# The factors of one elimination step side by side in SBUF instead of 128 bytes apart, in the 32 x 32 inverses of a chunked recurrence

## Chip, cores and metric

One core of one Trainium2 chip. The metric is the device time of one execution in microseconds (us), from the first to the last instruction of the kernel and what little lies around them; less is better.

## What is computed

A recurrence over 768 time steps (4 batches x 8 heads, head size 40), then two feed-forward blocks on its 3072 output rows.

```
for t in range(768):                       # per batch b and head h, state is 40 x 40
    y[t]  = r[t] @ state
    Sa    = state @ a[t]
    state = state * w[t][None, :] - outer(Sa, b[t]) + outer(v[t], k[t])
x = y as rows of 320
x = layer_norm(h * softmax(h)) * g_ln @ w_out        # h = x @ w_in, 1024 wide
out = leaky(x @ w_in2) @ w_out2                      # 2048 wide, slope alpha below 0
```

## The kernel before

The recurrence is cut into 24 chunks of 32 time steps. Within a chunk the steps depend on each other through a strictly lower triangular 32 x 32 matrix per batch and head; the kernel builds these matrices (`gen1`), inverts one plus them, and uses the inverses as matmul operands. Six calls of `inverse(W)`, W = 0 to 5, invert four chunks each: 128 triangular matrices of 32 x 32, of which every partition holds one, 1024 floats long. A chunk has a slot in the program; `slot(g)` writes down the recurrence's stages in a fixed order (`stage_x`, `stage_u`, `stage_uf`, `stage_st`, `stage_g2`, `stage_s`, `stage_y`), and strews work of other chunks between them: transposes (`trans`), `gen1` of later chunks, decoding of weights (`decode`), the first feed-forward block (`mm1`, `soft`, `mm2`) in a queue of TensorE work.

The order of TensorE's instructions is written out by hand, from tables of expected waits (`WT`) and expected durations; the other engines take theirs in the order of the program as the tile scheduler places it. Each engine runs its instructions in that order.

`inverse(0)` runs alone ahead of slot 0. `inverse(W)` for W = 1 to 5 has 33 pieces, a start, 31 steps and an end. The first 18 pieces are strewn over the slot g = 4W - 2, the rest over g = 4W - 1. The result is read by `stage_u` (L442) and `stage_uf` (L465) of the slots 4W to 4W + 3. So `stage_u` of slot 4W waits for the end piece.

- The start (L366) is a block transpose on VectorE (DVE): it reads `lraw`, laid out [row s][chunk and pair][column t] over partitions, and turns it so that each partition has one matrix `NT`.
- Step s adds to every row i <= s of the growing inverse `M` a multiple of the factors of that step: `M[i, t] += M[i, s] * NT[t, s]` for t > s. It is done as a product into `tmp` (L354) and a sum (L358), each over (s + 1) x (31 - s) elements, which is 87 elements at s = 2 and s = 28, 256 at s = 15. In the product the first operand is one word of `M` per row, repeated along the row, and the second is the list of factors, repeated for every row. The first two and the last two steps go another way (L383), with scalars from `NT` or `M`.
- The end (L387) is a second block transpose, of `M`, into the memory of `NT`.
- With W = 0, DVE takes only the rows below 10 and POOL the rest (`pool_rows`), and each product and sum on DVE is cut in two. With W > 0, DVE takes all rows; POOL only clears `M` and sets its diagonal (L132, L133).

Other instructions of DVE that come up below, in its order among the inverse's: L482 (state sums out of `pst`), L508 (`KBS` sums), L544 (`Yt`, the chunk's output out of `py`), L580 and L582 (the softmax of the first block), L620 (`lnl`).

Of the kernel before, what the change touches and what calls it, by code (L numbers as in the profile page):

```python
# [48 lines left out]
def tile_kernel(ctx: ExitStack, tc: tile.TileContext, w_fm, a0_fm, a_fm, kb_fm, r_fm, v_fm, v_tm,  # L49
                w1_in, w1_out, g_ln, w2_in, w2_out, alpha, ident_d, mask_d, r, k, v, w, a, b, w1_nat, out,  # L50
                manual=True):
    nc = tc.nc
# [78 lines left out]
    def unit(M, eng):  # L131
        eng.memset(M, 0.0)  # L132
        eng.memset(M.rearrange("p a b -> p (a b)")[:, ::33], -1.0)  # L133
# [22 lines left out]
    st = {}  # L156
# [185 lines left out]

    def inverse(W):
        M, NT = LMN[2 * W % 3], LMN[(2 * W + 1) % 3]

        P = PR[W > 0]

        def rank1(eng, tmp, s, rows):
            nt = 31 - s
            l = NT[:, s + 1:32, s]  # L350
            tv = tmp[:, 0:sum(b - a for a, b in rows) * nt].rearrange("p (i t) -> p i t", t=nt)
            for a, b in rows:
                sh = [128, b - a, nt]
                eng.tensor_tensor(out=tv[:, a - rows[0][0]:b - rows[0][0]], in0=M[:, a:b, s:s + 1].to_broadcast(sh),  # L354
                                  in1=l.unsqueeze(1).to_broadcast(sh), op=ALU.mult)
            for a, b in rows:
                o = M[:, a:b, s + 1:32]
                r = eng.tensor_tensor(out=o, in0=o, in1=tv[:, a - rows[0][0]:b - rows[0][0]], op=ALU.add)  # L358
            return r

        def pool_rows():
            for s in range(P, 31):
                rank1(nc.gpsimd, b1.tile([128, TM], F32, name="tmp2", tag="Yt"), s, [(P, s + 1)])

        def start():
            nc.vector.transpose(out=NT, in_=st["lraw", W].rearrange("p l t -> p t l"))  # L366
            if W:
                unit(M, nc.gpsimd)
            pool_rows()

        def step(s):
            n, nt = min(s + 1, P), 31 - s
            m = n // 2
            if n <= SM:
                ops = [(M[:, i, s + 1:32], NT[:, s + 1:32, s], M[:, i, s:s + 1]) for i in range(n)]
            elif nt <= SM:
                ops = [(M[:, 0:n, s + 1 + i], M[:, 0:n, s], NT[:, s + 1 + i, s:s + 1]) for i in range(nt)]
            else:
                st["step"] = rank1(nc.vector, b1.tile([128, 256], F32, name="tmp"), s,
                                   [(0, m), (m, n)] if W == 0 else [(0, n)])  # L380
                return
            for o, x, f in ops:
                st["step"] = nc.vector.scalar_tensor_tensor(out=o, in0=x, scalar=f, in1=o, op0=ALU.mult,  # L383
                                                            op1=ALU.add)

        def fin():
            st["fence"] = nc.vector.transpose(out=NT.rearrange("p l t -> p t l"), in_=M.rearrange("p i t -> p t i"))  # L387
            st["NT", W] = NT

        yield 1.1, start  # L390
        for s in range(31):
            yield 0.15 + 2 * (s + 1) * (31 - s) / 960.0, (lambda s=s: step(s))
        yield 1.1, fin
# [402 lines left out]
    def inv_tasks(g):  # L796
        W, c4 = divmod(g, 4)
        if 2 * W + 3 >= NW or c4 < 2:
            return []
        inv = [f for _, f in inverse(W + 1)]  # L800
        return inv[:NI] if c4 == 2 else inv[NI:]
# [115 lines left out]
    def phase1():  # L917
# [23 lines left out]
        for i, (_, f) in enumerate(inverse(0)):  # L941
            f()
            if i == KSTEP:
                with tc.issue_after(st["step"].ins):
                    nc.vector.memset(busy[:, 0:1], 0.0)  # L945
# [403 lines left out]
```

## Time and profile before

| | before |
|---|---|
| median of 3 runs | 1167.23 us (1165.36 to 1168.53) |
| the profiled execution, its own time | 1166.42 us |
| its span, first to last instruction | 1164.6 us |
| TensorE (PE) busy | 978.9 us (84%) |
| VectorE (DVE) busy | 811.2 us (70%) |
| ScalarE (ACT) busy | 520.4 us (45%) |
| GpSimd (POOL) busy | 503.7 us (43%) |
| mean granted TensorE clock | 0.901 of full speed |

A busy share is a mean over the whole span; the second feed-forward block (the last 410 us) is almost all TensorE, the stretch before it is mixed. The rows further down take single stretches.

### The profile page before, as it was taken

The numbers are of one execution on the slowest core, as the hardware profiler recorded it, in microseconds if no ns is written. First come the engines' busy times: TensorE is split into PE (matmuls) and PEld (weight loads), VectorE is DVE, ScalarE is ACT, GpSimd is POOL, SyncE is SP. The second block draws the span as 40 slices with busy tenths as digits, with TensorE's granted clock in tenths as the row PEclk, the third lists the DMA queues.
The fourth block names the chain that finished last, engine by engine and source line by source line (L and its number), as shares of the span: only waits on it lengthen the run. The fifth ranks groups of instructions, "written<-read, shape, count | busy, mean of one in ns | idle before, by whom it ended". The sixth has DMA issues, their size and how long they took to land.

```text
span 1164.6 us, 37097 instructions
## 1 busy us (share of the span) xinstructions
PE 978.9 (84%) x15934; PEld 808.5 (69%) x15934; DVE 811.2 (70%) x1610; ACT 520.4 (45%) x1198; POOL 503.7 (43%) x546
## 2 busy tenths in 40 slices
PE   7275687588878978888787878889999999999997
PEld 3143354467666767666676667778989999999997
DVE  8898689978997798779977976656533333333343
ACT  3325454476537653755475547556312121212121
POOL 6858455444434442443344234436233333333333
PEclk8687987789888887988888889999999999999999
DMA  7513343334333433343333342443402020201000
GB/s 161 149 53 85 99 137 113 99 104 120 106 97 107 122 80 96 90 100 111 99 85 88 101 135 71 117 141 133 124 2 61 8 62 7 62 6 41 6 23 15
DMA packets 104543, 99.52 MB, mean 85 GB/s; under 512 B 38068, under 2 KB 83764, under 8 KB 104372
## 3 DMA queue, kind: packets, MB, share of 16 engines
q1 hardware_dynamic: 104372, 97.07, 30.6%
q8 instruction: 127, 2.08, 0.8%
q14 instruction: 44, 0.36, 0.1%
HBM read 71.62 MB, written 25.43 MB: 83 GB/s over the span
## 4 chain that ended last, share of the span: by engine, by line
PE 47%; DVE 29%; POOL 7%; issue 6%; ACT 5%; DMA 5%; SPq 0%; POOLq 0%; DVEq 0%; ACTq 0%
PE ph L1015 15%; DVE tmp L354 5%; PE h L575 5%; PE acc L1035 5%; PE acc L1033 5%; PE acc L1034 5%; DVE LMN L358 4%; DMA kbf<-in_kb_fm_dram 4%; DVE VUS L482 2%; DVE KBS L508 2%; PE pf L465 2%; POOL XS L312 2%; DVE H L277 2%; PE po L628 1%; PE pu L442 1%
## 5 line engine op out<-in xcount | busy, mean ns | idle before, releaser
L1022 POOL TENSOR_TENSOR gll<-gt,gh 128x512 fp32r<-128x512 f32 (+1 forms) x112 | 129.0, 1152 | 224.0 <-ACT gh L1021 222.9
L595 DVE TENSOR_SCALAR gt<-ph,al 128x512 f32<-128x512 f32 (+1 forms) x112 | 75.4, 673 | 189.8 <-PE ph L1015 189.6
L1021 ACT CAST gh<-gt 128x512 fp32r<-128x512 f32 (+1 forms) x112 | 62.5, 559 | 254.5 <-DVE gt L596 212.6
L575 PE MATMUL h<-w1h,xt 128*128 128x512 f32 x240 | 105.2, 487 | 16.3 <-ACT h L584 16.3
L312 POOL TENSOR_TENSOR XS<-XS,H 40x512 f32<-40x512 f32 (+1 forms) x48 | 66.6, 1392 | 92.7 <-DVE H L277 55.8
L354 DVE TENSOR_TENSOR tmp<-LMN,LMN 128x87 f32<-128x87 f32 (+25 forms) x189 | 95.0, 514 | 3.4
L1033 PE MATMUL acc<-w2h,gh 128*128 128x320 f32 x288 | 89.0, 309 | 0.0
L1034 PE MATMUL acc<-w2l,gh 128*128 128x320 f32 x288 | 89.0, 309 | 0.0
L1035 PE MATMUL acc<-w2h,gll 128*128 128x320 f32 x288 | 88.9, 309 | 0.0
L528 POOL TENSOR_TENSOR YS<-YS,mask 64x512 f32<-64x512 f32 x48 | 64.0, 1333 | 49.0 <-ACT YS L527 47.2
L211 PE MATMUL busy<-busy 128*128 128x512 bf16 x221 | 66.4, 455 | 19.5 <-DVE busy L945 18.2
L358 DVE TENSOR_TENSOR LMN<-LMN,tmp 128x87 f32<-128x87 f32 (+25 forms) x189 | 76.3, 415 | 2.7
L596 DVE SCALAR_TENSOR_TENSOR gt<-ph,gt 128x512 f32<-128x512 f32 (+1 forms) x112 | 68.8, 615 | 3.7
L575 PE MATMUL h<-w1l,xt 128*128 128x512 f32 x144 | 68.6, 476 | 0.0
L575 PEld LDWEIGHTS h<-w1h,xt 128*128 128x128 f32 x240 | 50.3, 221 | 26.0 <-ACT h L584 18.5
L628 PE MATMUL po<-wo1h,lnh 128*128 128x320 f32 x192 | 67.1, 349 | 0.5 <-DVE lnl L620 0.5
L630 PE MATMUL po<-wo1h,lnl 128*128 128x320 f32 x192 | 61.9, 322 | 0.0
L629 PE MATMUL po<-wo1l,lnh 128*128 128x320 f32 x192 | 61.8, 322 | 0.0
L1015 PE MATMUL ph<-w1h,w2h 128*128 128x512 f32 x180 | 59.3, 394 | 0.0
L211 PEld LDWEIGHTS <-busy 128*128 128x128 bf16 x221 | 22.9, 112 | 49.7 <-DVE busy L945 18.3
L326 PE MATMUL pg<-XS,kbf 104*32 104x64 f32 x1536 | 38.5, 239 | 22.0 <-DVE kbf L303 12.8
L581 ACT ACTIVATE P<-h,sm 128x1024 f32<-128x1024 f32 x24 | 26.7, 1114 | 65.1 <-DVE sm L580 62.1
(200 smaller groups left out, 2743.5 us busy)
## 6 DMA issues: line engine op xcount, KB each, us to landing
kbf<-in_kb_fm_dram SPq DMA_DIRECT2D x24, 416.0 KB
x2d<-x SPq DMA_DIRECT2D x24, 320.0 KB
xd<-Y SPq DMA_DIRECT2D x24, 256.0 KB
xt<-xd SPq DMA_DIRECT2D x12, 512.0 KB
raw<-in_w_in_dram SPq DMA_DIRECT2D x20, 256.0 KB
wt<-in_w_fm_dram SPq DMA_DIRECT2D x24, 211.7 KB
raw<-in_w_in_dram SPq DMA_DIRECT2D x8, 512.0 KB
raw<-in_w_out_dram SPq DMA_DIRECT2D x16, 256.0 KB
```

What stands on the lines that cost most here:

```text
L211: nc.tensor.matmul(st["busy"], lhsT=busy[:, 0:128], rhs=busy, start=True, stop=True)
L312: (nc.vector if w < 2 and e in DA else nc.gpsimd).tensor_tensor(out=o, in0=o, in1=h, op=ALU.mult)
L354: eng.tensor_tensor(out=tv[:, a - rows[0][0]:b - rows[0][0]], in0=M[:, a:b, s:s + 1].to_broadcast(sh), in1=l.unsqueeze(1).to_broadcast(sh) ...
L358: r = eng.tensor_tensor(out=o, in0=o, in1=tv[:, a - rows[0][0]:b - rows[0][0]], op=ALU.add)
L575: nc.tensor.matmul(st["h"][:, ns], lhsT=l, rhs=r, start=j == 0, stop=j == len(ops) - 1)
L595: nc.vector.tensor_scalar(out=tmp, in0=h, scalar1=0.0, scalar2=al, op0=ALU.min, op1=ALU.mult)
L628: nc.tensor.matmul(po, lhsT=lh[:, k], rhs=wo1h[:, k], start=k == 0, stop=False)
L1015: nc.tensor.matmul(p, lhsT=l, rhs=r, start=j == 0, stop=j == len(ops) - 1)
L1022: nc.gpsimd.tensor_tensor(out=gll, in0=t, in1=f32(gh), op=ALU.subtract)
L1033: nc.tensor.matmul(acc, lhsT=gh[:, cs], rhs=oh, start=f == 0, stop=False)
L1034: nc.tensor.matmul(acc, lhsT=gh[:, cs], rhs=ol, start=False, stop=False)
L1035: nc.tensor.matmul(acc, lhsT=gll[:, cs], rhs=oh, start=False, stop=f == K2 - 1)
```

## The change

`NT` as an object in memory keeps its place and size. A view `N` with the two inner dimensions exchanged takes its place in the start and in the steps: the start's transpose writes matrix element [t][s] to word 32 s + t in place of word 32 t + s. The factors `N[:, s+1:32, s]` of one step are then 31 - s neighbouring words; before, they were 31 - s words with 32 words from one to the next. The end piece writes the result as before, and nothing else differs: on every engine the same instructions stand in the same order.

```diff
     def inverse(W):
         M, NT = LMN[2 * W % 3], LMN[(2 * W + 1) % 3]
+        N = NT.rearrange("p s t -> p t s")
...
         def rank1(eng, tmp, s, rows):
             nt = 31 - s
-            l = NT[:, s + 1:32, s]
+            l = N[:, s + 1:32, s]
...
         def start():
-            nc.vector.transpose(out=NT, in_=st["lraw", W].rearrange("p l t -> p t l"))
+            nc.vector.transpose(out=N, in_=st["lraw", W].rearrange("p l t -> p t l"))
...
             if n <= SM:
-                ops = [(M[:, i, s + 1:32], NT[:, s + 1:32, s], M[:, i, s:s + 1]) for i in range(n)]
+                ops = [(M[:, i, s + 1:32], N[:, s + 1:32, s], M[:, i, s:s + 1]) for i in range(n)]
             elif nt <= SM:
-                ops = [(M[:, 0:n, s + 1 + i], M[:, 0:n, s], NT[:, s + 1 + i, s:s + 1]) for i in range(nt)]
+                ops = [(M[:, 0:n, s + 1 + i], M[:, 0:n, s], N[:, s + 1 + i, s:s + 1]) for i in range(nt)]
```

## Rows read from the trace of the kernel before

**Rows 1.** The whole chain that ended last, by line; and the page's product group.

```profile
by line: PE ph L1015 14.8%; issue 6.1%; DVE tmp L354 5.5%; PE h L575 4.7%; PE acc L1035 4.7%; PE acc L1033 4.7%; PE acc L1034 4.7%; DVE LMN L358 4.4%; DMA kbf<-in_kb_fm_dram 3.6%; DVE VUS L482 2.0%; DVE KBS L508 1.8%; PE pf L465 1.7%; POOL 
...
L354 DVE TENSOR_TENSOR tmp<-LMN,LMN 128x87 f32<-128x87 f32 (+25 forms) x189 | 95.0, 514 | 3.4
```

**Rows 2.** Stretches with inverses: length, busy us by engine, clock, DMA (W 0, 1, 2, 3, 5).

```profile
core 0: us, PE busy (x) PEld busy (x) DVE busy (x) ACT busy (x) POOL busy (x), PEclk, DMA share, GB/s
36.00:69.00 33.00, 9.69 (x99) 4.49 (x100) 31.70 (x121) 6.60 (x21) 23.20 (x57) 0.64 0.37 95
161.00:225.00 64.00, 42.09 (x836) 27.89 (x833) 60.88 (x117) 23.98 (x56) 29.20 (x29) 0.73 0.37 105
284.00:336.00 52.00, 41.16 (x963) 33.17 (x965) 49.75 (x105) 28.57 (x70) 19.35 (x25) 0.90 0.38 99
398.00:453.00 55.00, 44.21 (x937) 36.36 (x939) 49.44 (x105) 28.48 (x69) 19.34 (x25) 0.84 0.37 92
...
635.00:689.00 54.00, 43.43 (x1014) 35.13 (x1009) 49.47 (x105) 28.18 (x69) 17.77 (x22) 0.86 0.41 110
```

**Rows 3.** TensorE's longest waits, 250 to 700 us: total, times, longest.

```profile
PE pu L442 <- DVE LMN L387: 18.3, 4, 5.4
...
PE px L429 <- DVE Yt L544: 9.7, 4, 2.7
```

**Rows 4.** Products and sums at s = 15, inverses 2 to 5: busy, mean ns.

```profile
L354 DVE TENSOR_TENSOR tmp<-LMN,LMN 128x256 f32<-128x256 f32 x4 | 2.5, 616 | 0.1
...
L358 DVE TENSOR_TENSOR LMN<-LMN,tmp 128x256 f32<-128x256 f32 x4 | 1.7, 426 | 0.1
```

**Rows 5.** DVE's order of time, inverse 2, s = 2, 27 and 28: start us, us.

```profile
288.95 0.30 DVE L354 TENSOR_TENSOR tmp<-LMN,LMN 128x87 f32<-128x87 f32 x1
...
330.48 0.37 DVE L354 TENSOR_TENSOR tmp<-LMN,LMN 128x112 f32<-128x112 f32 x1
330.88 0.28 DVE L358 TENSOR_TENSOR LMN<-LMN,tmp 128x112 f32<-128x112 f32 x1
331.19 0.25 DVE L354 TENSOR_TENSOR tmp<-LMN,LMN 128x87 f32<-128x87 f32 x1
331.48 0.25 DVE L358 TENSOR_TENSOR LMN<-LMN,tmp 128x87 f32<-128x87 f32 x1
```

**Rows 6.** The two block transposes, by line: duration ns min/median/max.

```profile
L366 DVE STREAM_TRANSPOSE LMN<-LMN x6: 1918/1982/2003, 36.1 to 635.9; 128x1024 f32<-128x1024 f32 x6
...
L387 DVE STREAM_TRANSPOSE LMN<-LMN x6: 1972/2017/2029, 66.0 to 685.8; 128x1024 f32<-128x1024 f32 x6
```

**Rows 7.** Order of time, inverse 2: TensorE's pst and py, DVE's L482 and L544.

```profile
313.54 1.42 PE L477 MATMUL pst<-VUS,KBS 64*40 64x40 f32 x64
...
315.30 0.49 DVE L482 TENSOR_TENSOR VUS<-pst,VUS 40x320 f32<-40x320 f32 x1
...
323.77 1.42 PE L540 MATMUL py<-YS,KBS 104*40 104x32 f32 x64
...
326.75 0.68 DVE L544 TENSOR_TENSOR Yt<-py,H 104x512 f32<-104x512 f32 x1
```

**Rows 8.** Waits of DVE in inverse 3, and of TensorE in inverse 1.

```profile
DVE Yt L544 <- PE py L540: 1.9, 1, 1.9
...
PE h L575 <- ACT h L584: 11.4, 1, 11.4
```

**Rows 9.** Order of time in inverse 0: DVE and POOL together.

```profile
52.08 0.66 DVE L354 TENSOR_TENSOR tmp<-LMN,LMN 128x85 f32<-128x85 f32 x2
52.66 0.62 DVE L358 TENSOR_TENSOR LMN<-LMN,tmp 128x85 f32<-128x85 f32 x2
...
51.85 0.52 POOL L354 TENSOR_TENSOR tmp<-LMN,LMN 128x121 f32<-128x121 f32 x1
52.45 0.57 POOL L358 TENSOR_TENSOR LMN<-LMN,tmp 128x121 f32<-128x121 f32 x1
```

## The prediction

> **What bounds the kernel now.** I read the chain of work that ended last first, to see whether the edited lines lie on it at all. They do [rows 1]: the products (L354) hold 5.5% of the span, 5.5% of 1164.6 = 64 us, out of 95.0 us that DVE spends on them in the whole run. So two thirds of what they cost is on the path, by this view.
>
> Next, the stretches in which inverses run [rows 2]. The reader is to see DVE's busy time against the length: 31.70 of 33 us in inverse 0, 60.88 of 64 in inverse 1, 49.75 of 52 in inverse 2, 49.44 of 55 in inverse 3, 49.47 of 54 in inverse 5. DVE is the engine that hardly ever idles there, while TensorE, which carries the next stages, is busy for some 80% of inverses 2 to 5, 66% of inverse 1.
>
> Third, what TensorE waits for in that part [rows 3]. It waits 18.3 us in four times at `pu` for the inverse's end piece, and 9.7 us in four times at `px` for `Yt`, which stands in DVE's order behind the first half of the inverse. Both waits end with a DVE instruction that has inverse steps ahead of it. In inverse 1 the wait has another name but the same cause [rows 8]: 11.4 us at `h` for ACT's L584, which needs DVE's L582, which stands behind the end piece.
>
> **The price of the 128-byte step.** The sum of a step (L358) works on as many elements as its product (L354), with neighbouring words in all operands. At s = 15 the two take 616 and 426 ns [rows 4]: 190 ns more for 256 elements, 0.74 ns each. The difference could come from the second operand (128-byte steps) or from the first (one word repeated along a row). Three rows speak for the second. At s = 27 (rows of 4 factors) product and sum take 0.37 and 0.28 us, 0.8 ns per element; at s = 28 (rows of 3 factors) 0.25 and 0.25 [rows 5]: with three factors read over and over the price is gone, though the first operand is repeated there as everywhere. And the start's transpose reads 1024 elements in 128-byte steps with no operand repeated, and takes 1982 ns [rows 6]. From the sums, 256 elements in 426 ns and 87 in 250, an element without the price takes 1.04 ns, so 1024 would take 426 + 768 x 1.04 = 1225; the 757 ns on top are 0.74 ns per element, the same price. So I charge 0.74 ns per element to the 128-byte read, for s = 2 to 27.
>
> [...]
>
> **What the change removes.** One inverse with W > 0 has 5187 product elements in s = 2 to 27 (the sum of (s + 1)(31 - s)); at 0.74 that is 3.84 us of DVE time, 19.2 us over five. What of it reaches the end differs by place. In inverse 2:
>
> - Before `Yt` of the first slot, s = 2 to 8: 1064 elements, 0.79 us. TensorE waits at `px` for this `Yt`, 9.7 / 4 = 2.4 us each time [rows 3], so all of it counts.
> - s = 9 to 18: 2455 elements, 1.82 us. Here TensorE runs beside DVE: `pst` ends at 313.54 + 1.42 = 314.96 and DVE takes it up at 315.30 [rows 7]. DVE could come 0.34 us earlier before it waits for TensorE. Counted: 0.34, and the other 1.48 us turn into idle time of DVE.
> - s = 19 to 27: 1668 elements, 1.24 us, in front of the end piece, for which TensorE waits 18.3 / 4 = 4.6 us [rows 3]. The second `Yt` stands among them, and its `py` is ready at 325.19, 1.56 us before DVE comes to it [rows 7]; the 0.94 us of the steps s = 19 to 24 ahead of it fit in that. Counted: all 1.24.
>
> That makes 2.4 us. Inverse 5 has the same look, 2.4. In inverse 3 DVE already waits 1.9 us for `py` at that second `Yt` [rows 8], so of the last part only the steps behind it count, s = 25 to 27 (403 elements, 0.30 us): 0.79 + 0.34 + 0.30 = 1.4. Inverse 4, whose rows I don't show, lies between, 2.0. In inverse 1 DVE is busy in all but 3 of 64 us and TensorE waits much; of 3.84 I count 2.4, since decoding of weights, which also needs ACT, POOL and transfers, shares the stretch. Sum: 2.4 + 2.4 + 1.4 + 2.0 + 2.4 = 10.6 us.
>
> **Inverse 0.** DVE has at most 10 rows: 3534 elements in s = 2 to 27, at 0.74 2.6 us, and nothing else runs on DVE. But product and sum differ little while POOL works beside it: two products of 85 elements take 0.66 us, two sums 0.62 [rows 9], 0.04 us for 170 elements, 0.24 ns each, 0.8 us in all. Something of POOL's, whose own product of 121 elements lasts 0.52 us in the same time, covers most of the price. Between 0.8 and 2.6 I take 1.3, nearer to the row of the same place. POOL's products read the factors too; their 0.52 against 0.57 us of the sums shows no price, so I count nothing (at 0.74 on its 1771 elements, the sum of (s - 9)(31 - s) for s = 10 to 30, 1.3 us would be the other end).
>
> **What it adds.** The start's transpose now writes in 128-byte steps as well as it reads so. The end piece does both already and takes 2017 ns against 1982 [rows 6]: 0.035 us, six times, 0.2 us (0.7 us by the extremes, 2029 against 1918). The steps of L383 read factors in the first two steps only, 91 elements in an inverse, 0.07 us less: nothing. No wait, buffer or transfer is added, and no order changes.
>
> **Sum.** 10.6 + 1.3 - 0.2 = 11.7 us off the profiled execution's 1166.42, 1154.7. The median of before lies 0.8 us above that execution, so 1155.5. Bounds: all of 19.2 + 2.6 on the path gives 1167.2 - 21.8 = 1145.4; only the steps ahead of the first `Yt` and behind the second in inverses 2 to 5, 4 x (0.79 + 0.30) = 4.4 us, gives 1162.8.
>
> **The rivals.**
>
> *The repeated word pays as well* (8%). Then the price hangs on the first operand, the products stay at 616 ns, and the time stays at 1167.2 or 0.2 above, for the transposes. For it: the rows of s = 15 and s = 27 fit it as well. Against it: s = 28, and the transposes. [...]
>
> *TensorE closes the gap* (10%). DVE's time falls by 19 us, but the stages' matmuls take over as the bound: what `pu` gains is waited for again further on in the slot, and only the gain at `px` is left, 4 x 0.79 = 3.2 us, 1164.0. For it: in inverses 2 to 5 TensorE is busy for 80% already, and the middle steps gain next to nothing. Against it: the waits at `px` and `pu` are 2 to 5 us each, larger than what is taken from them.
>
> *The clock eats it* (6%), which ends slower. [...]
>
> **How the numbers follow.** My forecast, a gain of 4 to 18 us, has 76%: 1149 to 1163. The first two rivals together stand at 18%, the slower one at 6%. The likeliest is 1155.5; the range 1149 to 1163.5 holds about 8 in 10. A difference under 0.3% (3.5 us) can't be told from none on this kernel. Faster by more: 0.80, since some of the second rival ends just beyond. Within: 0.13. Slower: 0.07.
>
> **What would show it.** The product at 256 elements falls from 616 to about 430 ns (by the first rival it stays above 600), that of 87 elements at s = 28 stays at 0.25 us, that at s = 2 falls from 0.30 to 0.25. The start's transpose stays near 2.0 us. DVE's busy time falls by about 20 us, and DVE shows new idle time at L482 of the second slots, some 1.5 us each, which is where the rest of the price went. TensorE's wait at `pu` falls by 1 to 1.5 us each time, that at `px` by 0.8. From slot 20 on (680 us before) everything stands 11 to 12 us earlier, and the last 410 us are as before. I am wrong in the price if the products don't fall to the sums' level; in the path if they do and the time doesn't follow; in inverse 0 if its DVE stretch of 32 us loses less than 0.8 or more than 2.6 us.

## The result and the profile after

The changed kernel takes 1148.59 us (median of 6 runs, 1143.54 to 1149.97) against 1166.11 for the kernel before beside it: ratio 0.985, interval 0.9817 to 0.9884, so 17.5 us less. A second series of it gave 0.984 (0.9804 to 0.9876). The forecast was 11.7 us less and a range down to 1149.0. The direction and the price of the step hold; the size was too small. Of the 6.9 us between the forecast time, 1155.5, and 1148.59, 1.1 us is the base: the forecast started from a median of 1167.23. The profiled execution took 1149.97 us with a span of 1148.2, against 1166.42 and 1164.6.

All line numbers behind L343 are one higher than before. First the page of the changed kernel, busy time by engine, and its two groups of products and sums.

```profile
PE 976.5 (85%) x15913; PEld 810.8 (71%) x15934; DVE 790.7 (69%) x1610; ACT 519.9 (45%) x1198; POOL 496.7 (43%) x546
...
L359 DVE TENSOR_TENSOR LMN<-LMN,tmp 128x87 f32<-128x87 f32 (+25 forms) x189 | 75.9, 413 | 2.7
L355 DVE TENSOR_TENSOR tmp<-LMN,LMN 128x87 f32<-128x87 f32 (+25 forms) x189 | 71.9, 392 | 3.4
```

The products fell from 95.0 us [rows 1] to 71.9, 23.1 us less, below the sums. DVE's busy time as a whole fell by 20.5. The grouped rows of s = 15 show the price gone to the last element, and the order of time in inverse 2 shows the ends of the row lengths (s = 2, and s = 27 and 28); these answer to [rows 4] and [rows 5].

```profile
L355 DVE TENSOR_TENSOR tmp<-LMN,LMN 128x256 f32<-128x256 f32 x4 | 1.7, 426 | 0.1
L359 DVE TENSOR_TENSOR LMN<-LMN,tmp 128x256 f32<-128x256 f32 x4 | 1.7, 424 | 0.1
```

```profile
285.92 0.23 DVE L355 TENSOR_TENSOR tmp<-LMN,LMN 128x87 f32<-128x87 f32 x1
...
324.84 0.28 DVE L355 TENSOR_TENSOR tmp<-LMN,LMN 128x112 f32<-128x112 f32 x1
325.15 0.28 DVE L359 TENSOR_TENSOR LMN<-LMN,tmp 128x112 f32<-128x112 f32 x1
325.46 0.25 DVE L355 TENSOR_TENSOR tmp<-LMN,LMN 128x87 f32<-128x87 f32 x1
```

616 ns became 426, with the first operand a repeated word as before; 0.37 us became 0.28 where a row has four factors, and 0.25 stayed 0.25 where it has three. So the repeated word costs nothing here: the product that has it takes 426 ns, the sum that has none 424. The 128-byte step was the whole price.

The same stretches as in [rows 2], from the start piece to the end piece:

```profile
core 0: us, PE busy (x) PEld busy (x) DVE busy (x) ACT busy (x) POOL busy (x), PEclk, DMA share, GB/s
38.00:67.00 29.00, 8.88 (x96) 4.03 (x98) 27.55 (x120) 6.46 (x20) 18.52 (x50) 0.59 0.37 98
161.00:222.00 61.00, 40.62 (x801) 28.66 (x802) 56.10 (x117) 23.76 (x56) 26.83 (x29) 0.70 0.39 110
281.00:330.00 49.00, 40.24 (x972) 32.86 (x974) 45.89 (x105) 28.33 (x70) 19.01 (x25) 0.93 0.41 104
393.00:442.00 49.00, 41.02 (x947) 33.48 (x948) 45.68 (x105) 28.50 (x69) 19.06 (x25) 0.91 0.40 103
622.00:671.00 49.00, 40.15 (x944) 32.52 (x942) 45.44 (x102) 27.39 (x66) 16.85 (x22) 0.90 0.43 119
```

DVE's busy time falls by some 4 to 5 us in each stretch, with as many instructions as before, give or take three. TensorE's share of its stretch rises a little (40.24 of 49 us in inverse 2, 41.16 of 52 before). The clock in inverses 2, 3 and 5 is higher in this execution (0.93, 0.91 and 0.90 against 0.90, 0.84 and 0.86), in inverses 0 and 1 lower (0.59 and 0.70 against 0.64 and 0.73).

TensorE's waits, to be read beside [rows 3]:

```profile
PE pu L443 <- DVE LMN L388: 16.5, 4, 4.9
...
PE px L430 <- DVE Yt L545: 8.9, 4, 2.4
```

They fell by 1.8 and 0.8 us in total; the prediction wanted 4 to 6 and 3.2. Both ends of the wait moved: in inverse 2 the end piece stands 2.6 us closer to the start piece (the table of stretches below), yet the wait for it lost about 0.5, so TensorE comes to it earlier too. The experiments bear this out: the total at `pu` is 17.9 to 18.4 us in the six profiles in which the late steps, from s = 19 on, have the 128-byte step, and 16.1 to 16.5 in the eight in which they read neighbours, whatever the earlier steps do. So here the change in a wait's length is no gauge of what a faster releaser is worth.

The last 410 us are as before: TensorE is busy for 397.06 us of them at a clock of 0.99 now, for 397.15 at 1.00 before. Of the inverse's instructions the start piece alone got longer, by 0.13 us in the median (1982 ns [rows 6] to 2111):

```profile
L367 DVE STREAM_TRANSPOSE LMN<-LMN x6: 2077/2111/2203, 38.3 to 622.7; 128x1024 f32<-128x1024 f32 x6
```

### The profile page after: what moved, and what is told of

It reads as the page before. It is cut to its first block, busy times and chain, and to the rows that moved or that the text cites. A ratio compares the mean times of both kernels' runs of the same rounds, so it can differ in the third digit from the quotient of the medians.

```text
span 1148.2 us, 37076 instructions
## 1 busy us (share of the span) xinstructions
PE 976.5 (85%) x15913; PEld 810.8 (71%) x15934; DVE 790.7 (69%) x1610; ACT 519.9 (45%) x1198; POOL 496.7 (43%) x546
## 4 chain that ended last, share of the span: by engine, by line
PE 49%; DVE 29%; ACT 6%; issue 6%; POOL 5%; DMA 4%; SPq 0%; DVEq 0%; POOLq 0%; ACTq 0%
PE ph L1016 15%; PE h L576 5%; PE acc L1036 5%; PE acc L1035 5%; PE acc L1034 5%; DVE LMN L359 4%; DVE tmp L355 3%; DMA kbf<-in_kb_fm_dram 3%; DVE VUS L483 2%; DVE H L277 2%; PE pf L466 2%; DVE KBS L509 2%; DVE XS L336 2%; DVE kbf L303 1%; PE pg L326 1%
## 5 line engine op out<-in xcount | busy, mean ns | idle before, releaser
L211 PE MATMUL busy<-busy 128*128 128x512 bf16 x200 | 60.1, 454 | 24.6 <-DVE tmp L355 19.6
L355 DVE TENSOR_TENSOR tmp<-LMN,LMN 128x87 f32<-128x87 f32 (+25 forms) x189 | 71.9, 392 | 3.4
```

The source lines that it names most:

```text
L211: nc.tensor.matmul(st["busy"], lhsT=busy[:, 0:128], rhs=busy, start=True, stop=True)
```

## The experiments

Apart from `again` and `v_rows`, all of these take the changed kernel and put the 128-byte step back for chosen steps, inverses or engines. Only the products change (L355 of the changed kernel); the few scalar steps (L384) stay as changed. The products then read words of the same tile that lie across the diagonal, so these kernels compute with other factors; sizes, strides and order are those of the kernels compared. The edit is one line and a condition:

```diff
+    def old(W, s, eng):
+        return W > 0 and 9 <= s <= 18          # u_mid; the others differ here alone
...
-            l = N[:, s + 1:32, s]
+            l = (NT if old(W, s, eng) else N)[:, s + 1:32, s]
```

**The changed kernel once more (again), no edit.**

> The changed kernel once more, to know its time better and to have a second profile. If chance of the runs made the gap between 11.7 us forecast and 17.5 measured, this comes out near 1154; if not, near 1148.6 again. The stretch of inverse 0 is 28.3 us long again, the lengths of the slots with the second halves of inverses 1 to 5 vary between 24 and 29 us.

1148.8 us, 0.984 (0.9804 to 0.9876). Chance of the first series is out; the forecast was too small. The stretch of inverse 0 is 28.5 us in this profile.

**All products put back, the start as changed (u_all): `return True`.**

> The changed kernel with the 128-byte step put back in all products of all inverses (values differ, sizes and order are the same); only the start's transpose still writes in 128-byte steps, as changed. If nothing but the products' reads made the gain, this is the time of the kernel before plus six times 0.12 us for the longer start, 1166.8. If the four parts put back one by one (about 11 us by their medians) are all that there is, 1148.6 + 11 = 1159.6.

1165.97 us, 0.9997 (0.9974 to 1.0020). So the reads of the products are the whole gain, to within the 2.7 us of the interval, and the longer write of the start can't be seen in the time. This kernel computes with other factors than the kernel before and takes the same time, so the values don't disturb these comparisons by more than that. The four parts put back singly, below, come to some 10 us by their medians but to 2.3%, 26 us, by their ratios: time alone can't add them up.

**Inverse 0 put back (u_inv0): `return W == 0`.**

> The changed kernel with the 128-byte step put back in inverse 0 alone, on DVE and on POOL (values differ, sizes and order are the same). By the prediction's account 1.3 us slower than the changed kernel, 1149.9. By the rival, that the two engines share something and POOL's own price comes back as well, the stretch of inverse 0, which is 28.3 us long in the changed kernel and 31.9 in the one before, is 31.9 again, and the time 3.6 us more, 1152.2.

1152.21 us, 0.9911 (0.9877 to 0.9945), and in its trace the stretch from the start piece to the end of the end piece is 32.2 us. The lengths come from the order of time of DVE, here of the kernel before, of the changed kernel and of this one:

```profile
36.13 1.92 DVE L366 STREAM_TRANSPOSE LMN<-LMN 128x1024 f32<-128x1024 f32 x1 [1.19 <-ACT LMN L339]
...
65.97 2.03 DVE L387 STREAM_TRANSPOSE LMN<-LMN 128x1024 f32<-128x1024 f32 x1
```

```profile
38.27 2.12 DVE L367 STREAM_TRANSPOSE LMN<-LMN 128x1024 f32<-128x1024 f32 x1 [1.19 <-ACT LMN L339]
...
64.47 2.06 DVE L388 STREAM_TRANSPOSE LMN<-LMN 128x1024 f32<-128x1024 f32 x1
```

```profile
38.78 2.11 DVE L370 STREAM_TRANSPOSE LMN<-LMN 128x1024 f32<-128x1024 f32 x1 [1.20 <-ACT LMN L339]
...
69.01 2.00 DVE L391 STREAM_TRANSPOSE LMN<-LMN 128x1024 f32<-128x1024 f32 x1
```

65.97 + 2.03 - 36.13 = 31.9 us, 64.47 + 2.06 - 38.27 = 28.3, 69.01 + 2.00 - 38.78 = 32.2. Inverse 0 is worth some 3.6 to 4 us, not 1.3, and more than the upper bound of 2.6 that I had put on DVE's side of it. (By the ratios it would be 0.7%, 8 us, with 6 to either side; by the medians 3.6.)

The other profiles give the same lengths, and those of inverses 1 to 5 as well. Each is taken from the start of the start piece to the end of the end piece, in us, over all profiles but that of v_rows in which every product of that inverse has the 128-byte step, and over those in which none has:

| inverse | 0 | 1 | 2 | 3 | 4 | 5 |
|---|---|---|---|---|---|---|
| with the step | 31.9 to 32.3 | 54.2 to 55.1 | 50.4 to 52.0 | 51.8 to 54.3 | 50.5 to 51.4 | 50.1 to 52.2 |
| profiles | 6 | 3 | 3 | 3 | 3 | 3 |
| without | 28.3 to 28.5 | 52.0 to 52.4 | 47.8 to 48.2 | 48.0 to 51.8 | 48.6 to 52.5 | 47.1 to 48.2 |
| profiles | 6 | 5 | 5 | 5 | 5 | 5 |
| means, shorter by | 3.6 | 2.3 | 3.0 | 2.8 | 0.2 | 3.8 |

Inverse 0 runs alone ahead of slot 0, and its 3.6 us stand clear of the scatter. So do the differences of inverses 1, 2 and 5; those of 3 and 4 don't.

**POOL's products of inverse 0 alone (u_pool): `return W == 0 and eng is nc.gpsimd`.**

> The changed kernel with the 128-byte step put back in POOL's products of inverse 0 alone (values differ, sizes and order are the same); DVE's products read neighbouring words. If POOL's reads have no price, as the prediction had it, the stretch of inverse 0 stays 28.3 us. If POOL pays 0.74 ns on each of its 1771 elements and DVE and POOL take turns, it becomes 28.3 + 1.3 = 29.6 us. If POOL sets the pace of both and DVE's price was hidden behind it, it becomes 31.9 as before.

1148.69 us, 0.984 (0.9804 to 0.9875): too little for the time. The stretch shows it:

```profile
35.79 2.05 DVE L370 STREAM_TRANSPOSE LMN<-LMN 128x1024 f32<-128x1024 f32 x1 [1.20 <-ACT LMN L339]
...
63.16 2.01 DVE L391 STREAM_TRANSPOSE LMN<-LMN 128x1024 f32<-128x1024 f32 x1
```

63.16 + 2.01 - 35.79 = 29.4 us, 1.1 more than 28.3, close to the 29.6 of the rival. POOL pays for the step too (its 21 products take 421 ns in the mean, 377 in the changed kernel), and DVE, which ends last, feels it.

**DVE's products of inverse 0 alone (u_dve0): `return W == 0 and eng is nc.vector`.**

> The changed kernel with the 128-byte step put back in DVE's products of inverse 0 alone; POOL's read neighbouring words (values differ, sizes and order are the same). The stretch of inverse 0 was 28.3 us with no such step, 29.4 with POOL's alone, 31.9 with both. If DVE and POOL take turns and each one's price adds, DVE's 3534 x 0.74 = 2.6 us make 30.9. If DVE's price is covered by POOL's work, as the row of two products in 0.66 us let the prediction think, it stays under 29.5, and the two only cost 3.5 us together.

A single run: 1146.3 us, which says nothing at this size. The stretch, and what DVE and POOL do in its middle:

```profile
36.45 2.03 DVE L370 STREAM_TRANSPOSE LMN<-LMN 128x1024 f32<-128x1024 f32 x1 [1.20 <-ACT LMN L339]
...
52.92 0.61 DVE L358 TENSOR_TENSOR tmp<-LMN,LMN 128x85 f32<-128x85 f32 x2
...
65.70 2.04 DVE L391 STREAM_TRANSPOSE LMN<-LMN 128x1024 f32<-128x1024 f32 x1
...
52.02 0.60 POOL L362 TENSOR_TENSOR LMN<-LMN,tmp 128x120 f32<-128x120 f32 x1
52.70 0.47 POOL L358 TENSOR_TENSOR tmp<-LMN,LMN 128x117 f32<-128x117 f32 x1
```

65.70 + 2.04 - 36.45 = 31.3 us, 3.0 more than 28.3. With POOL's 1.1 that makes 4.1; both together cost 3.9. The prices add, within some 0.3 us. That fits the expectation by which the two engines take turns; whether they do, and at what, no run shows. The step of one engine shows in the other's rows as well: the POOL sums here, which are unchanged, take up to 0.60 us for 120 elements and 436 ns in the mean of all 21, against 383 ns in the changed kernel, where they look like this, with DVE's rows of the same middle ahead of them:

```profile
52.59 0.51 DVE L355 TENSOR_TENSOR tmp<-LMN,LMN 128x85 f32<-128x85 f32 x2
53.02 0.61 DVE L359 TENSOR_TENSOR LMN<-LMN,tmp 128x85 f32<-128x85 f32 x2
...
50.73 0.47 POOL L355 TENSOR_TENSOR tmp<-LMN,LMN 128x121 f32<-128x121 f32 x1
51.27 0.47 POOL L359 TENSOR_TENSOR LMN<-LMN,tmp 128x121 f32<-128x121 f32 x1
```

**Inverses 1 to 5 put back (u_w): `return W > 0`.**

> The changed kernel with the 128-byte step put back in all products of inverses 1 to 5, inverse 0 as changed (values differ, sizes and order are the same). The prediction put 10.6 us on these five inverses: 1148.7 + 10.6 = 1159.3. If the whole gain of 17.3 us less the 3.5 of inverse 0 is theirs, 1162.5.

1164.15 us, 0.9973 (0.9946 to 1.0001). Against the 0.984 of the changed kernel that is 1.33%, 15.5 us for the five inverses, with some 5 us to either side by the two intervals. The other way to the same quantity, from all put back (0.9997) to inverse 0 put back (0.9911), gives 0.86%, 10.0 us, give or take 5. The forecast of 10.6 is compatible with both; so is 14. The stretches in the table above narrow it: the five sum up to 260.6 us with the step and 248.5 without, in the mean, 12.0 less, give or take some 4.

**Parts of inverses 1 to 5 put back: s = 2 to 8 (u_first, `s <= 8`), 9 to 18 (u_mid), from 19 on (u_tail).**

> The changed kernel with the 128-byte step put back in the products of s = 2 to 8 of inverses 1 to 5 alone (these read other words of the same tile, so the values differ; sizes and order are the same). DVE gets back 1064 x 0.74 = 0.79 us per inverse. Both accounts say that all of it counts, since TensorE waits at px behind it: 5 x 0.79 = 3.9 us slower than the changed kernel, about 1152.5 us. If the time is within 1 us of the changed kernel's, these steps are not on the path.

> The changed kernel with the 128-byte step put back in the products of s = 9 to 18 of inverses 1 to 5 alone (values differ, sizes and order are the same). DVE gets back 2455 x 0.74 = 1.82 us per inverse. By the prediction's account only 0.34 us of it reaches the end in inverses 2 to 5, and most of it in inverse 1: about 3 us slower than the changed kernel, 1151.5. By the rival, that all of DVE's time counts, 5 x 1.82 = 9.1 us slower, 1157.7.

> The changed kernel with the 128-byte step put back in the products from s = 19 on of inverses 1 to 5 alone (values differ, sizes and order are the same). DVE gets back 1668 x 0.74 = 1.24 us per inverse, in front of the end piece. By the prediction's account 1.24 + 0.30 + 1.0 + 1.24 us in inverses 2 to 5 and some 0.9 in inverse 1: 4.7 us slower than the changed kernel, 1153.3. By the rival that all counts, 6.2 us, 1154.8: no difference that this run could tell.

**The same parts done alone, all else put back (o_first, o_mid, o_tail): `return W == 0 or s > 8`, and so on.**

> All products with the 128-byte step but those of s = 2 to 8 of inverses 1 to 5 (values differ, sizes and order are the same). With all put back the time was 1166.0. By the prediction these steps are worth 5 x 0.79 = 3.9 us, 1162.1, and the slots with the first halves get 0.8 us shorter. Putting back these steps alone cost nothing; if they are worth nothing, 1166.

> All products with the 128-byte step but those of s = 9 to 18 of inverses 1 to 5 (values differ, sizes and order are the same). By the prediction's account about 3 us less than 1166.0, 1163, since TensorE is as late as DVE at the next meeting; if all of DVE's time counts, 9.1 us less, 1156.9. Putting them back alone cost 3 to 5 us.

> All products with the 128-byte step but those from s = 19 on of inverses 1 to 5 (values differ, sizes and order are the same). By the prediction 4.7 us less than 1166.0, 1161.3; the wait at pu gets 0.9 to 1.2 us shorter each time. If DVE only comes to the second Yt earlier and waits there, 1.5 us less, 1164.5.

| part | put back alone | worth | done alone | worth | forecast |
|---|---|---|---|---|---|
| s = 2 to 8 | 1147.89, 0.9866 (0.9829 to 0.9902) | 0.26% | 1164.88, 0.9972 (0.9948 to 0.9996) | 0.25% | 3.9 us |
| s = 9 to 18 | 1151.62, 0.9905 (0.9869 to 0.9942) | 0.65% | 1162.96, 0.9958 (0.9937 to 0.9979) | 0.39% | about 3 us |
| s = 19 to 28 | 1152.49, 0.9905 (0.9876 to 0.9933) | 0.65% | 1162.57, 0.9969 (0.9941 to 0.9997) | 0.28% | 4.7 us |

(Worth: ratio less the 0.984 of the changed kernel, or 0.9997 less the ratio.) The three sum up to 1.56% one way and 0.92% the other, 18 and 11 us, around the 10 to 15.5 of all five inverses together. Each worth has 0.3 to 0.5% to either side, 4 to 6 us, so none can be told from its forecast, and they can't be put in order. The first steps show it best: 1147.89 us lies within 1 us of the changed kernel, which was to mean that they are not on the path, while both ratios point to some 3 us; that stays open. Medians and ratios differ because the kernel before had a median of 1164.88 us beside the parts put back and 1166.28 beside the changed kernel's second series.

**A version with the 128-byte step left in the end piece's write (v_rows).**

This one starts from the kernel before. ACT writes `lraw` in another order, and `M` is kept turned, so that the first operand of a product is a row of `M`, read over and over, and the second one repeated factor per row. The first two steps, 91 elements in an inverse, still move in 128-byte steps.

```diff
-                nc.scalar.activation(out=lraw[r:r + 32, c4 * 8:c4 * 8 + 8, :], in_=pg[o + 32:o + 64, :, e],
+                nc.scalar.activation(out=lraw[r:r + 32, :, c4 * 8:c4 * 8 + 8],
+                                     in_=pg[o + 32:o + 64, :, e].rearrange("p s t -> p t s"),
...
+                eng.tensor_tensor(out=v, in0=M[:, s:s + 1, a:b].to_broadcast(sh),
+                                  in1=NT[:, s + 1:32, s:s + 1].to_broadcast(sh), op=ALU.mult)
...
-            nc.vector.transpose(out=N, in_=st["lraw", W].rearrange("p l t -> p t l"))
+            nc.vector.transpose(out=NT, in_=st["lraw", W])
...
-            st["fence"] = nc.vector.transpose(out=NT.rearrange("p l t -> p t l"), in_=M.rearrange("p i t -> p t i"))
+            st["fence"] = nc.vector.transpose(out=NT.rearrange("p l t -> p t l"), in_=M)
```

> A version with no 128-byte step on DVE but the end piece's write: ACT writes lraw in the order in which the start reads it, M is kept turned, so that a step reads a row of M over and over and one factor per row. The start should take 426 + 768 x 1.04 = 1225 ns in place of 2111, 0.9 us less in each of six inverses, the end piece 1980. If all of the start's gain counts, 1148.6 - 5.3 = 1143.3; if ACT's reads of PSUM in 256-byte steps make its L339 (376 ns before) longer, the start begins later and the gain is gone: 1148 or more.

1146.46 us, 0.9829 (0.9793 to 0.9864), which can't be told from the changed kernel's 0.984, nor from the 1143.3 that was expected if all of the start's gain counts. Its rows, by line, of ACT's writes, the start and the end:

```profile
L339 ACT ACTIVATE LMN<-pg x96: 372/376/380, 22.6 to 615.3; 32x256 f32<-32x256 f32 x96
...
L366 DVE STREAM_TRANSPOSE LMN<-LMN x6: 1233/1245/1247, 37.1 to 615.7; 128x1024 f32<-128x1024 f32 x6
...
L387 DVE STREAM_TRANSPOSE LMN<-LMN x6: 1905/1908/1917, 62.8 to 660.2; 128x1024 f32<-128x1024 f32 x6
```

The start came down to 1245 ns, near the 1225 worked out from the sums; ACT's writes in the new order cost what the old ones did, 376 ns in the median. The price shows a third time, 737 ns for 1024 elements against the 1982 of before, 0.72 ns each, on an instruction that the change left dear.

## Why the prediction was right and where it was too small

**The price: right.** 0.74 ns per element, on the second operand, with three factors free (0.25 us for product and sum at s = 28). 616 ns became 426 for 256 elements, and the start without the step 1245 for a forecast of 1225. The first rival, that the repeated word pays as well, is out: with that word still in place the product takes 426 ns, the sum 424.

**The whole gain is the reads: right.** All put back is the time before (0.9997, within 0.23%).

**Inverse 0: the term that was mis-sized.** The prediction took 1.3 us, between 0.8 and 2.6, "nearer to the row of the same place", and counted nothing for POOL. Measured: 3.6 us from profile to profile, 3.9 from the changed kernel to u_inv0; 3.0 of DVE's products, 1.1 of POOL's, taken singly. That is beyond the 2.6 us by which the prediction said it would know itself wrong here. The step that failed is the yardstick: two products of 85 elements against two sums in the same stretch, 0.66 and 0.62 us [rows 9]. Both had POOL beside them, and a sum that is itself drawn out (two of 85 elements in 0.62 us, where one of 87 took 0.25 in inverse 2 [rows 5]) shows no difference to a product. The changed kernel's rows there are 0.51 us for the two products and 0.61 for the two sums: the products fell by 0.15 us, 0.9 ns per element, and stand below the sums. For the same reason POOL's 0.52 against 0.57 us said nothing of its price; both are 0.47 in the changed kernel. The yardstick for both was in [rows 4], far off, but undisturbed.

**Inverses 1 to 5: 10.6 us forecast, 10 and 15.5 by the times, 12.0 by the stretches.** The account by meetings with TensorE gave the right size, as far as the scatter lets one see. Over the profiles of the table DVE's busy time in the five stretches falls by 18.7 us in the mean (19.2 forecast), of which 12.0 make the stretches shorter and 6.7 turn into idle time of DVE (8.6 forecast). In inverse 2 the middle steps can be followed. From the start piece to the first L482 (now L483) of the second slot it took 315.30 [rows 7] - 284.64 = 30.66 us before and takes 311.12 - 281.52 = 29.60 now, 1.06 less; 0.79 + 0.34 less the longer start was forecast, 1.0. Here are the start piece of before, and of the changed kernel the start piece and the places where DVE is idle on the way to L483:

```profile
284.64 1.97 DVE L366 STREAM_TRANSPOSE LMN<-LMN 128x1024 f32<-128x1024 f32 x1 [0.85 <-ACT LMN L339]
```

```profile
281.52 2.11 DVE L367 STREAM_TRANSPOSE LMN<-LMN 128x1024 f32<-128x1024 f32 x1 [0.85 <-ACT LMN L339]
...
304.75 0.42 DVE L647 TENSOR_TENSOR x<-ptx,x 128x256 fp32r<-128x256 f32 x1 [0.27 <-ACT x L646]
...
309.89 0.69 DVE L621 TENSOR_TENSOR lnl<-ptr,lnh 128x512 fp32r<-128x512 f32 x1 [0.29 <-ACT lnh L620]
311.12 0.49 DVE L483 TENSOR_TENSOR VUS<-pst,VUS 40x320 f32<-40x320 f32 x1 [0.21 <-PE pst L478]
```

The idle time did not come where the prediction put it, some 1.5 us at L482 of the second slot: here 0.21 us waits for `pst` and 0.56 for ACT. Whether the five inverses are worth more than 10.6 stays open; neither the intervals nor the scatter of the stretches settles it.

**The clock: priced only as a loss.** I had it as the rival that ends slower, at 6%. No run shows the clock eating the gain. The twelve timed runs of the changed kernel had a mean granted clock of 0.906, those of the kernel before beside the experiments 0.900. Over 180 timed runs of all fourteen versions, a line fitted with one constant for each version gives 0.43 us less for each 0.001 of mean clock; in u_w alone the runs go from 1158.54 us at 0.909 to 1170.63 at 0.895, though its fastest, 1156.54, had 0.900. At an equal clock the fit leaves 15.1 us, give or take 1.7, of the gain. But this does not make the other 2.8 us a gift of the clock. The mean is taken over the whole span, and it rises by arithmetic alone when time at a low clock is taken out: 17.5 us out at 0.60, about the clock of inverse 0's stretch (0.64 and 0.59 above), would give, by estimate, (1166.1 x 0.900 - 17.5 x 0.60) / 1148.6 = 0.905. Whether the change raised the clock of any stretch was not tried and is not shown.

**The start: 0.2 us forecast, 0.8 measured** (6 x 0.13), with no trace in the time.

By terms: 11.7 forecast, and 2.3 more for inverse 0, make 14.0. By the stretches it is 3.6 for inverse 0 and 12.0 for inverses 1 to 5, the longer start included: 15.6 of 17.5. The other 2 us are not placed: in the profiles above the start piece of inverse 0 alone stands anywhere from 35.79 to 38.78 us, and the stretches from one inverse to the next differ by up to 1.9 us between the two kernels' profiles.

**What the forecast said would show:** products at the sums' level, s = 28 unchanged, DVE 20 us less, the last 410 us as before: all seen. Not seen: the new idle time at L482 (DVE's waits for `pst` there sum up to 9.1 us in five, 7.5 in three before), and a loss of inverse 0 within 0.8 to 2.6 us. The waits at `pu` and `px` fell by less than forecast although the time fell by more: wrong in kind, as said above.

## What to carry to other kernels

In fp32, lay a factor list that is read over and over so that its words are neighbours: here one 128-byte step in an inner loop cost DVE 0.74 ns per element, 45% on top of a 256-element product, while repeating one word cost nothing (426 ns against 424 of the sum), and POOL's products paid as well (421 ns in the mean against 377). Take the price of a stride from an undisturbed stretch, against an instruction that isn't itself drawn out; a difference read where two engines draw out each other's instructions can hide most of it (0.24 ns per element here in place of 0.74). And count a saving meeting by meeting with the engine that waits: of the 18.7 us that DVE lost in the five strewn inverses, some 12 made their stretches shorter. The length of a single wait at `pu` moved by far less, from 4.6 to 4.1 us in the mean, since both of its ends moved.

## What the runs showed of the hardware that was not expected

- The granted clock goes with the scatter. Three of four slots of the changed kernel with the same work, from one `px` to the next (the columns are those of the stretches above):

```profile
297.60:321.70 24.10, 22.34 (x514) 17.89 (x517) 22.46 (x56) 17.82 (x44) 11.14 (x14) 0.86 0.38 89
...
521.80:550.20 28.40, 27.58 (x514) 22.10 (x514) 23.23 (x55) 17.72 (x44) 10.88 (x14) 0.65 0.31 75
639.90:663.70 23.80, 22.16 (x514) 17.62 (x514) 22.35 (x56) 17.74 (x44) 9.90 (x12) 0.86 0.41 120
```

  With 514 matmuls each, 24 us at 0.86 and 28.4 at 0.65: the slot at 0.65, whose clock was 0.50 from 521.8 to 538 us and 1.00 from 542 on, took 4 us more, as much as DVE saves in a whole inverse.
- Three words, 128 bytes apart and read in turn, cost no more than neighbours (0.25 us for product and sum alike [rows 5], s = 28); four did (0.37 us against 0.28 of the sum, s = 27).
- DVE and POOL, both on two operands in SBUF, drew out each other's instructions in inverse 0: POOL's sums took 383 ns in the mean, or 436 with the step in DVE's products (u_dve0); DVE's products took 245 and 250 ns in two profiles of the changed kernel, 261 with the step in POOL's (u_pool).
- A block transpose of 1024 elements took 1245 ns in the median with neighbouring words on both sides (v_rows), 1908 with the step in the write alone (v_rows), 1982 in the read alone (the kernel before), and 1994 to 2111 in both (the two kernels): 663 and 737 ns singly, 749 to 866 together, so the prices hardly add.
